# A new order of turns for a gated linear attention kernel with an MLP

## The chip, the cores and the metric

One core of a Trainium2 chip runs the kernel. Its engines are TensorE (PE in the profile, its weight loads PEld), VectorE (DVE), ScalarE (ACT), GpSimd (POOL) and SyncE (SP), which here issues nearly all DMAs. Each engine works off its own queue of instructions in the order in which the program emits them; semaphores make one wait for another. The metric is the device time of one execution in microseconds, the median of several runs.

## The reference

Two blocks, one after the other, in float32 (the weights come as float64):

```python
for t in range(S):            # B=4, H=8, S=768, D=48
    state = alpha[:, :, t, :, None] * state + einsum('bhd,bhe->bhde', k[:, :, t], v[:, :, t])
    y[:, :, t] = einsum('bhd,bhde->bhe', q[:, :, t], state)
x = y.transpose(0, 2, 1, 3).reshape(B, S, H * D)      # (4, 768, 384)
xn = (x - mean) / sqrt(var + 1e-6) * g_ln
out = x + maximum(xn @ w_ch1, 0) @ w_ch2              # 384 -> 1536 -> 384
```

## The kernel before

The sequence of 768 steps is cut into six chunks of 128 rows; with the four batches that makes 24 pieces of attention, called tokens here and lettered a to x (chunk 0 is a to d, chunk 1 e to h, and so on). The work of a token is a Python generator, `attention(c, b)` from L294: its instructions are emitted in pieces, each ended by a `yield`. Every other part of the kernel is a generator as well. One piece of a generator is a turn. The order of the work is a string, ORDER, of 1508 letters, and this loop at the end of the kernel is all that schedules it:

```python
with tc.manual_schedule():
    for turn in ORDER:
        next(turns[turn], None)
```

Each letter runs the next turn of its generator. Since engines take their instructions in order of emission, the string fixes the order on every engine, SyncE's DMA issues included, and with it which buffer each tile gets: buffers rotate among a few (six PSUM banks of tag "bank" for nearly all results of TensorE, seven buffers for raw inputs, eleven of tag "sum"), and a tile that takes a used buffer waits for its last reader.

The letters:

- **a to x**, the tokens. In order: issue loads of q, k, v (first chunk alone; later ones are loaded by an earlier token at L135, L141, L153 and L169); logarithm of alpha (ScalarE, L308); running sums by a triangular matmul (TensorE, L313, L316 or, for a later token, L403); two exponentials (ScalarE, L320); products with k and q (VectorE, L323, L325); the row of gates to DRAM (L330). Then q and k are transposed: in chunks 0 and 1 by TensorE (L351) with copies, from chunk 2 on by VectorE (L362) and a way through DRAM, four issues out (L368, tile td) and four back (L375, tiles kT and qT). Then the scores (TensorE, L393 or L401), their mask (VectorE, L407 or L413), the gates back from DRAM (L419), the sums of k times v (TensorE, L428), the state (VectorE L441, GpSimd L443), the outputs (TensorE, L454 or L459 and L463), their copy to x (ScalarE, L474 or L486, with VectorE L482 or L489), x to DRAM (L498), the layer norm (ScalarE, for chunk 0 VectorE L511), and its transpose: TensorE (L522) up to chunk 3, VectorE (L528) and DRAM (L532, L535) after that.
- **A to L**, twelve pieces of the weights: a load (L203), then three steps on VectorE, one on ScalarE (L223) and more on VectorE (L225 to L232), which turn float64 into float32.
- **Y, Z, P, Q**, the MLP of chunk 0: 12 hidden products for each half of the batches (L558, ReLU at L561), and the second products (L570, L574).
- **S, W, X, N**, sums and differences of blocks on VectorE (L800 of w1, L634 of w2, L825 of the normalised x, L661 of the hidden values), for chunks 1 to 5, whose two matrix products are made with fewer block products than the plain ones.
- **1 and 2**, the first product of chunks 1 to 5: 15 block products for each half of the hidden rows. An even turn is the matmuls (L848), the next reads the PSUM bank: one step on VectorE or ScalarE, and for some of them one or two late additions on GpSimd (L867 to L887). **R and U** are the ReLUs of the two halves (ScalarE, L898).
- **M**, the second product: 20 block products for each of the five chunks, turn by turn matmuls (L674) and reading (L684, L687, and late additions on GpSimd at L690), with the result sent to DRAM (L549) as it is ready. **O** loads x back from DRAM for the residual (L545).

A turn that waits holds up everything that stands behind it on its engine. So TensorE, which has the most work, waits when an operand is late, or when the bank that it is to write has not been read.

Of the kernel before, what the change touches and what calls it, by code (L numbers as in the profile page):

```python
# [30 lines left out]


ORDER = (
    "baabaccacdaadaabcacdbbbaaacbbbbcefdcabacccaabcdefabeafAbaBeebfefcaccedbcebCaaeea"
    "ddAdcbcgdabdeccBdbhedeggfbfgagdfgaCfcbhfddfgccdghdbhhedhbhgddAhehdedgiccfefdfgjA"
    "ijhchigYBYiCZYfjBiBZhfZZYZiYfiZefYgZjZCYkfgYeEZADihgDgjjjYDfZeEegZDgijefCYfYheEZ"
    "lYgigGYihijZGYefFZYlEkefGZFkhghYfFSZZYijZYljkFZeHYeihHYggkYllGHlYZfZhZglZeIlSQSh"
    "hYiSJQYkggkHISgiJSgISlmkmIfPjnJfkSKPZlnjjnnQnhPjnnLhhlOPKjKkLklLkhnOmkWkkOWhQhOk"
    "PSljmmQhmmpjmXkSSiPXSjoWnlQQKjXkiPikmSjpXWk1Q2inlk1WXSXWoXm2olSmmnmpoX121Xooj2km"
    "p2oom21j1nmp112k122Xjq212k1SOWm2p11p2Olpj22P22kmWmi2nn1lrml2j1k21nWjm11ll1Si1n12"  # L40
    "1p1kRUWnomR22rnp2Xq2n1pn2OUrrrRoUooo1ooqlrrMM12N11opomMpotWmpMrnq21lMmqRlNqqlpUq"
    "mpRoM1NUs2iN2MMoorNMMNlMNpMmsMONMMqMpRrlWMNWNMtMUrMiNtqqqqMtrtttstXMNMMvMnMsNMss"
    "tNM1MoiMpiqqiMsqMONXMNXMsMXXMMMOMn12qXtXor2tqXs2qprrov121X1qrX1oputr1v1p22pvv2pu"
    "12MrssssvXrv2s2noru12oss2s21ts21nus121JvO22Uux2pnu1u12u121v1R2U121Rt2us2t1xw2OU1"
    "1Rn112ssNpt1trM2pR22sMuv1uuwuwRtrvstsN2XNrM1MMNUMUNx1MMxNNRwwNMvMM1XwtXMwNtUMMMM"
    "qqMMNwMXNMMMMMNMxrMNMqXONM2MMNxXNMwMXMxrMMMMXMXMXt2112u22q2tu21s2uvwt2xuv2xuMt22"
    "2ruw222wtv21111qr1wxwxXwsv2x1xswu1Uw1t221q1121v12112U1R12xvO1Rxw1121OUq121RURxMq"
    "2wM2211NMrxxNMUu1MMtXxRMvNXxMMNxN2M2XNNNMMMONwXMvUMRNxMwuNMuMMMMMNMwXvMMMNwMvMMN"
    "MOXMXMvXwMNxM1NMXMMMMw22222xO221x1122Xu1222v1u2121211111X1Ux2Ov2112112111R122211"
    "1v2w2211RUUMUu211R222XN2RMU2XMMXX1X1RXMXMMMXNMMN11RM1NX12NMNN1121N111U1O1X2M2NNM"  # L50
    "N2111XMMM1MMLMNR12N22121M11MM1M111MMM2M22NNM2MMN222M212MU2M2MRM12RU2MOOMM222M1OR"
    "2UMNMUMMM1NMURNMM2NMNNNNMN2OMNMMMUMMMRMMMNMMMMMNMMMNMMMNMMNMMMNMMMMM"
)


# [904 lines left out]
```

## Time and profile before

| | |
|---|---|
| median of 3 runs | 424.13 us (422.38 to 424.32) |
| profiled execution, its own time | 422.32 us |
| its span, first to last instruction | 420.5 us |
| TensorE busy | 409.4 us, 4608 matmuls |
| VectorE busy | 351.7 us |
| ScalarE busy | 178.0 us |
| GpSimd busy | 152.1 us |
| DMA | 61.26 MB, mean 146 GB/s |
| clock granted to TensorE | 1.00 |

The span is what the profiler records between the first and the last instruction; the profiled execution's own time is 1.8 us longer. Each matmul in float32 stands as two in the counts. The end of a matmul is modelled by the profiler, so gaps between TensorE's instructions are read from the list of waits and from the chain of work that ended last, rather than from the busy share alone.

### The profile page before, as it was taken

The page shows a single profiled execution, that of the slowest core. Times are in us where ns is not written, and L with a number is a line of the kernel's source. Part 1 is how long each engine was busy: PE and PEld are TensorE (multiplying, and loading weights), DVE is VectorE, ACT ScalarE, POOL GpSimd, SP SyncE. Part 2 cuts the span into 40 slices and gives each one's busy share as a digit, 9 for nine tenths or more (in the row PEclk, how much of TensorE's full clock was granted, in tenths as well). Part 3 has the DMA queues.
Part 4 walks back from the last instruction along what each step waited for, and adds up shares of the span by engine and source line. Part 5 has one row for each costly group of instructions (what it writes and reads, how often), then busy time and mean ns, then how long its engine had stood idle before and what let it go on. Part 6 is the DMA issues. An engine that isn't in the chain of part 4 may idle for free.

```text
span 420.5 us, 11553 instructions
## 1 busy us (share of the span) xinstructions
PE 409.4 (97%) x4608; PEld 361.1 (86%) x4608; DVE 351.7 (84%) x713; ACT 178.0 (42%) x440; POOL 152.1 (36%) x164
## 2 busy tenths in 40 slices
PE   7998999999999999999999999999999999999997
PEld 5887888766678889898889998888998899999996
DVE  4999999999999999977798985787975789856773
ACT  6598356654055476227456315224623233103210
POOL 1021111000304990133396033683151951369114
PEclk9999999999999999999999999999999999999999
DMA  8999899899768788586776234642017110002101
GB/s 267 320 294 308 205 259 302 237 200 199 194 181 201 190 170 211 102 229 170 166 171 156 40 98 105 123 117 76 1 59 154 44 48 2 0 19 82 51 20 56
DMA packets 135037, 61.26 MB, mean 146 GB/s; under 512 B 90908, under 2 KB 131100, under 8 KB 134984
## 3 DMA queue, kind: packets, MB, share of 16 engines
q1 hardware_dynamic: 134440, 60.37, 56.0%
q8 instruction: 36, 0.59, 0.6%
q10 hardware_dynamic: 544, 0.17, 0.2%
q14 instruction: 17, 0.14, 0.1%
HBM read 43.12 MB, written 17.39 MB: 144 GB/s over the span
## 4 chain that ended last, share of the span: by engine, by line
PE 77%; DMA 9%; DVE 7%; SPq 4%; issue 2%; ACT 1%; POOL 1%; DVEq 0%; ACTq 0%; POOLq 0%
PE ops L674 30%; PE hps L848 28%; PE ops L570 6%; DMA vn<-in_v_dram 2%; PE aps L401 2%; PE yps L459 2%; PE sums L428 2%; SPq L375 2%; PE yps L463 1%; DMA rq<-in_q_dram 1%; PE tps L351 1%; DMA gate<-row 1%; DMA ws<-in_moe_w_ch_dram 1%; SPq L368 1%; PE aps L393 1%
## 5 line engine op out<-in xcount | busy, mean ns | idle before, releaser
L690 POOL TENSOR_TENSOR ob<-ob,u 128x192 f32<-128x192 f32 x40 | 26.4, 670 | 81.7 <-DVE ob L687 62.2
L848 PE MATMUL hps<-sum,w 128*128 128x256 f32 x192 | 46.1, 381 | 0.0
L443 POOL TENSOR_TENSOR mid<-mid,gate 112x192 f32<-112x192 f32 x20 | 12.8, 640 | 89.9 <-DVE mid L441 70.8
L898 ACT ACTIVATE hT<-hT 128x512 f32<-128x512 f32 x48 | 28.9, 626 | 33.6 <-POOL hT L870 16.2
L848 PEld LDWEIGHTS hps<-sum,w 128*128 128x128 f32 x192 | 36.1, 190 | 4.9
L674 PE MATMUL ops<-w,hT 128*128 128x192 f32 x224 | 40.3, 326 | 0.0
L674 PEld LDWEIGHTS ops<-w,hT 128*128 128x128 f32 x224 | 37.1, 190 | 0.5
L848 PE MATMUL hps<-xT,w 128*128 128x256 f32 x136 | 34.6, 381 | 1.0 <-ACT x L474 1.0
L570 PE MATMUL ops<-w,hT 128*128 128x384 f32 x96 | 33.0, 491 | 0.0
L558 PE MATMUL hps<-xT,w 128*128 128x256 f32 x144 | 32.7, 383 | 0.0
L674 PE MATMUL ops<-ws,sum 128*128 128x192 f32 x160 | 29.2, 329 | 1.5 <-ACT x L486 1.5
L558 PEld LDWEIGHTS hps<-xT,w 128*128 128x128 f32 x144 | 26.9, 190 | 3.9
L848 PEld LDWEIGHTS hps<-xT,w 128*128 128x128 f32 x136 | 25.2, 190 | 4.4 <-ACT x L474 1.4
L674 PEld LDWEIGHTS ops<-ws,sum 128*128 128x128 f32 x160 | 26.3, 190 | 2.4 <-ACT x L486 1.8
L570 PEld LDWEIGHTS ops<-w,hT 128*128 128x128 f32 x96 | 17.7, 190 | 10.7
L684 DVE TENSOR_TENSOR ob<-ops,ob 128x192 f32<-128x192 f32 x50 | 17.6, 352 | 10.4 <-PE ops L674 5.7
L674 PE MATMUL ops<-ws,hT 128*128 128x192 f32 x128 | 23.7, 328 | 0.0
L459 PEld LDWEIGHTS yps<-st,qT 48*64 48x64 f32 x320 | 20.0, 134 | 3.9 <-issue 2.1
L463 PE MATMUL yps<-vx,at 64*64 64x48 f32 x320 | 23.0, 219 | 0.0
L463 PE MATMUL yps<-vn,at 64*64 64x48 f32 x320 | 22.5, 220 | 0.0
L459 PE MATMUL yps<-st,qT 48*64 48x48 f32 x320 | 22.1, 220 | 0.1
L674 PE MATMUL ops<-more,sum 128*128 128x192 f32 x120 | 22.0, 326 | 0.0
(248 smaller groups left out, 1115.7 us busy)
## 6 DMA issues: line engine op xcount, KB each, us to landing
ws<-in_moe_w_ch_dram SPq DMA_DIRECT2D x12, 768.0 KB, 6.0
td<-tr SPq DMA_DIRECT2D x64, 96.0 KB, 2.8
vn<-in_v_dram SPq DMA_DIRECT2D x12, 384.0 KB
kept<-x SPq DMA_DIRECT2D x24, 192.0 KB, 4.3
ob<-kept SPq DMA_DIRECT2D x24, 192.0 KB, 2.5
out_dram<-ob SPq DMA_DIRECT2D x19, 192.0 KB, 2.5
ra<-in_alpha_dram SPq DMA_DIRECT2D x16, 192.0 KB, 2.5
kT<-td SPq DMA_DIRECT2D x32, 96.0 KB, 4.4
```

The source lines that it names most:

```text
L375: nc.sync.dma_start(t[64 * i:64 * i + D].rearrange("r p s t -> r p (s t)"), td[n, :, i].rearrange("p d t -> d p t"))
L401: nc.tensor.matmul(to, kT[rs, p, s], qT[rs, p, s], start=True, stop=True)
L443: nc.gpsimd.tensor_mul(new, new, by)
L459: nc.tensor.matmul(yps[i][halves[s], i, p], qT[rs, p, s], (now, mid)[s][rs, p], start=True, stop=r != i)
L463: nc.tensor.matmul(yps[r][halves[s], i, p], at[halves[r], p, s], by, start=r != i, stop=True)
L558: nc.tensor.matmul(hps, w1[:, j // 2, f, j % 2 * P:][:, :P], xT_of[0][:, f, bs], start=(f == 0), stop=(f == NF - 1))
L570: nc.tensor.matmul(ops_of[b], hT_of[c][:, j, b], w2[:, j], start=(j == 0), stop=(j == NJ - 1))
L674: nc.tensor.matmul(acc, lhs[:, j], rhs[:, j], start=(j == 0), stop=(j == NT - 1))
L684: nc.vector.tensor_add(x, acc, x)
L690: getattr(nc.gpsimd, f"tensor_{op}")(x, x, y)
L848: nc.tensor.matmul(acc[:, i], w, b, start=True, stop=True)
L898: nc.scalar.activation(out=x, in_=x, func=AFT.Relu)
```

## The change

The change replaces the string ORDER by another with the same 1508 letters, each as often as before. No function, buffer, transfer or instruction is added or taken away. The two strings agree letter by letter in 74 places; a turn is moved by 12 places on average, the farthest by 359. Both strings end on turns of M, N and a few others.

```diff
 ORDER = (
-    "baabaccacdaadaabcacdbbbaaacbbbbcefdcabacccaabcdefabeafAbaBeebfefcaccedbcebCaaeea"
-    "ddAdcbcgdabdeccBdbhedeggfbfgagdfgaCfcbhfddfgccdghdbhhedhbhgddAhehdedgiccfefdfgjA"
-    "ijhchigYBYiCZYfjBiBZhfZZYZiYfiZefYgZjZCYkfgYeEZADihgDgjjjYDfZeEegZDgijefCYfYheEZ"
-    "lYgigGYihijZGYefFZYlEkefGZFkhghYfFSZZYijZYljkFZeHYeihHYggkYllGHlYZfZhZglZeIlSQSh"
...
-    "1Rn112ssNpt1trM2pR22sMuv1uuwuwRtrvstsN2XNrM1MMNUMUNx1MMxNNRwwNMvMM1XwtXMwNtUMMMM"
...
-    "2UMNMUMMM1NMURNMM2NMNNNNMN2OMNMMMUMMMRMMMNMMMMMNMMMNMMMNMMNMMMNMMMMM"
+    "bacabcadaacbcaadbcadabcababbebaccbadbaaBbccaedcbceAeeaaacbfecfBcdafddeaedbdeafae"
+    "bcdccbfgadhAdcgCcdbebeebfhggdfgbfffbCdcgfgecdfchgdfhgabcddchdhAiiegjhacehedhhjfg"
+    "biAdfidAeBhBijffYYiCjZZYYifZYlZCgjYDlYYjjZZYBZYgDieEgDgDjZZekEhZYGZgZigZGeeYgYgg"
+    "fZYEhfGfkChihiYFYijfgEhgkhFZYhgYfghijgkFeZZlGZShfZYHlhHfYFYZeZHelYiZgllPmZkJIgJk"
...
+    "Us1pXqU11x2tO2MM1vwMUM12xuRvu1vurNNNNwtOuuMwRxvNtxRNutwwMM2MOwNXwMNuXMMtNM1rMMMw"
...
+    "MNM1MMOMRMNMUUM2ONMNNNMO2MMMUMNMMMMMRMMNNMMMNMNMMNMMMMMMMMNMNMMMMMMM"
 )
```

More of the change, by code (lines that the diff above doesn't have):

```diff
@@ L33 @@
 ORDER = (
-    "baabaccacdaadaabcacdbbbaaacbbbbcefdcabacccaabcdefabeafAbaBeebfefcaccedbcebCaaeea"
-    "ddAdcbcgdabdeccBdbhedeggfbfgagdfgaCfcbhfddfgccdghdbhhedhbhgddAhehdedgiccfefdfgjA"
-    "ijhchigYBYiCZYfjBiBZhfZZYZiYfiZefYgZjZCYkfgYeEZADihgDgjjjYDfZeEegZDgijefCYfYheEZ"
-    "lYgigGYihijZGYefFZYlEkefGZFkhghYfFSZZYijZYljkFZeHYeihHYggkYllGHlYZfZhZglZeIlSQSh"
-    "hYiSJQYkggkHISgiJSgISlmkmIfPjnJfkSKPZlnjjnnQnhPjnnLhhlOPKjKkLklLkhnOmkWkkOWhQhOk"
-    "PSljmmQhmmpjmXkSSiPXSjoWnlQQKjXkiPikmSjpXWk1Q2inlk1WXSXWoXm2olSmmnmpoX121Xooj2km"
@@ L40 @@
[L40 to L44, printed above, removed]
-    "1Rn112ssNpt1trM2pR22sMuv1uuwuwRtrvstsN2XNrM1MMNUMUNx1MMxNNRwwNMvMM1XwtXMwNtUMMMM"
@@ L46 @@
[L46 to L51, printed above, removed]
@@ L52 @@
-    "2UMNMUMMM1NMURNMM2NMNNNNMN2OMNMMMUMMMRMMMNMMMMMNMMMNMMMNMMNMMMNMMMMM"
+    "bacabcadaacbcaadbcadabcababbebaccbadbaaBbccaedcbceAeeaaacbfecfBcdafddeaedbdeafae"
+    "bcdccbfgadhAdcgCcdbebeebfhggdfgbfffbCdcgfgecdfchgdfhgabcddchdhAiiegjhacehedhhjfg"
+    "biAdfidAeBhBijffYYiCjZZYYifZYlZCgjYDlYYjjZZYBZYgDieEgDgDjZZekEhZYGZgZigZGeeYgYgg"
+    "fZYEhfGfkChihiYFYijfgEhgkhFZYhgYfghijgkFeZZlGZShfZYHlhHfYFYZeZHelYiZgllPmZkJIgJk"
+    "PeiYjJIflHeSZIQgkIlYSjiPkffennSQlOKjLSnSjmSQhKnSjLnKPkiljnhSQnLkkjkWknkShOmPhkhl"
@@ new lines @@
+    "kOOhWlmmphmQmkmXjWQnXjlSQjPmkilXSXkP2OXWjXQjkjW2iXoSWX2oWX22Pi2mnol1j1mom2omSpoo"
+    "l1XSpk2oW2m112p1m2pm11m1W211pp12O122r22jnn21lpnmnjSml1riOn2l12Rl111kqS1m21W1Rkp2"
+    "o21mUXpq1mU2rUrnmj1rl2Rno2oomqonrormpokO1rNM2Mipin1op1ionoqUM2qp2W12RkMmNqiMoRtk"
+    "UrpkqNM1NoMliMlNUMMNMNMKNqMlNorMWrnmtltNRMsqppMWNMriMMMpNlsqqqnoqttNttMtMsXMMssM"
+    "sMNMNMX1oXXppMvstM2MXMMNMsppXoMXoqMsMMXM1nqqv11Xq1trMq2tqX21rn12v1r2ur2r222rvsqs"
+    "svsu1rs1nuvvt2s11ss11p22rtsvosn2uropuXru222221uts212stnU1211u1121222Op1Rp2tRU21R"
@@ new lines @@
+    "Us1pXqU11x2tO2MM1vwMUM12xuRvu1vurNNNNwtOuuMwRxvNtxRNutwwMM2MOwNXwMNuXMMtNM1rMMMw"
+    "qtXMMMxNUNxtMMsNMMMxXxMtXtrMMqMNrMXNvutMMwNuMMMNMMMxMLMOM11vvuq2X2O2wMus1wX11222"
+    "2r2Xt1222w22utsqxvw2x2ww1vx21sX12121xwvq2O2x2w111u1uvU121w12s1wuRvx12U11J1q21R1U"
+    "OvRxU121wMMu2xxsRNMw2NNMRM1MUNN2MMuUMqXN1MrNNRMNvMXNXMMMM2MMMxNM1uNXMMNMNMOXMXMv"
+    "MMXOMMMXxNxwxMMvNMMMMMXMx21w1x222212v12w222x122w2212X11UX2212121121121wx111MU11X"
+    "2RR2v1211212211R1URU211XOUM2XNRX1MX1RM2MXN2MXNXNMXXMXMMMN111U1MN1M1122MNM1MM2MM1"
@@ L53 @@
+    "11NNN121O11NM1MM21N1112N1122M1MMM12MM12N222M22M2RM1M2N22MM2MU1ON2M22M2UURR22RNNM"
+    "MNM1MMOMRMNMUUM2ONMNNNMO2MMMUMNMMMMMRMMNNMMMNMNMMNMMMMMMMMNMNMMMMMMM"
 )
```

## The prediction

> **What bounds the kernel now.** I read the page first, then the busy time by stretch, then TensorE's own waits, then the chain and the engines' timelines around each wait.
>
> ```profile
> span 420.5 us, 11553 instructions
> PE 409.4 (97%) x4608; PEld 361.1 (86%) x4608; DVE 351.7 (84%) x713; ACT 178.0 (42%) x440; POOL 152.1 (36%) x164
> ...
> PEclk9999999999999999999999999999999999999999
> ```
>
> TensorE has 11.1 us of idle time in 420.5, at full clock throughout. The change touches no instruction, so the 409.4 us stay, and only these 11.1 us, and what a new order adds to them, can move. The stretches (columns: window, length, busy time of each engine, clock, DMA share, GB/s) say where they lie:
>
> ```profile
> 0.00:20.00 20.00, 17.07 (x176) 13.11 (x176) 13.37 (x36) 11.11 (x25) 2.04 (x6) 1.00 0.93 303
> 20.00:180.00 160.00, 155.91 (x2372) 128.10 (x2373) 155.19 (x290) 86.88 (x219) 41.06 (x43) 1.00 0.85 216
> 180.00:400.00 220.00, 218.94 (x1960) 202.86 (x1959) 172.06 (x362) 78.59 (x194) 102.58 (x105) 1.00 0.37 91
> 400.00:420.50 20.50, 17.52 (x108) 17.03 (x106) 11.05 (x28) 1.47 (x3) 6.46 (x10) 1.00 0.11 39
> ```
>
> 2.9 us at the start, 3.0 at the end, 4.1 from 20 to 180 us, 1.1 after that. From 20 to 180 us VectorE (third figure) is as full as TensorE: 155.2 against 155.9 of 160 us. Behind 180 us VectorE has 22% to spare. TensorE's waits by name:
>
> ```profile
> PE xps L522 <- DVE xn L511: 1.9, 1, 1.9
> PE ops L674 <- ACT x L486: 1.5, 1, 1.5
> PE lps L250 <- DVE more L247: 1.1, 1, 1.1
> PE hps L848 <- ACT x L474: 1.0, 1, 1.0
> PE lps L313 <- ACT la L308: 1.0, 2, 0.5
> PE tps L351 <- DVE qk L325: 0.9, 1, 0.9
> ```
>
> The third, fifth and sixth are the start (first loads, first transpose), about 3.0 us. The other three, 1.95, 1.50 and 1.03 us, are what an order can win. The chain shows what the 1.50 comes from:
>
> ```profile
> 173.28 4.19 DMA ra<-in_alpha_dram
> 177.49 0.52 ACT la L308
> 178.02 0.20 ACT few L514
> 178.24 0.71 ACT xn L515
> 178.94 0.38 ACT x L486
> 179.33 0.04 issue
> 179.37 1.57 PE ops L674 x8
> ```
>
> A load of alpha took 4.19 us. ScalarE stood at its Ln, and behind the Ln stood the copy of x that frees a PSUM bank for the next product. And the 1.03 us:
>
> ```profile
> 284.90 1.23 POOL hT L886
> 286.14 0.02 issue
> 286.16 0.04 ACT hT L898
> ...
> 286.70 0.61 ACT hT L898
> 287.31 0.34 ACT x L474
> 287.66 0.04 issue
> 287.70 1.13 PE hps L848 x4
> ```
>
> GpSimd's late additions hold two ReLUs on ScalarE, and the copy of x that frees the bank stands behind them.
>
> **The change part by part.** I write k8 for the turn of token k with count 8, from 0. Against each string I count the TensorE work ahead of a turn: 1.30 us for a product of eight matmuls at L674, 0.86 for four at L848, 1.29 for six at L558, 2.58 for eight at L570 (all rows of the chain), and a token's small turns likewise. This is a place in the queue, not a time.
>
> *Loads of alpha, k, q (L169) ahead of their Ln.* Before, the load for s stands 0.3 us of TensorE work ahead of s0, that for o 0.8, that for v 1.3 (the wait above); the median of the twelve is 6.0. After, the smallest two are 2.6 (m, r), the next 7.4 (v), the median 11.1. Against the 4.19 us of the row, the wait at 177 us goes: gain 1.50, bounds 0 (the bank comes late for another reason) and 1.50. I take 1.5. Next late there is the load for r: its issue can run ahead of its place by some 3 us, as SP did before (below), and I charge nothing; without that cover it costs 4.2-2.6 = 1.6.
>
> *ReLUs and GpSimd (U15, R15, x16).* Before, turn 1-85 stands ahead of 2-85, so U15 waits for the third of four additions, and U15 and R15 both stand ahead of x16. After, 2-85 comes first, and x16 stands behind U15 but ahead of R15. Two GpSimd additions of 1.23 and 1.27 us are no longer ahead of U15, so the bank comes 2.5 us earlier: gain 1.0, bounds 0 and 1.03.
>
> *The transposes at 31 us (b21, C1, b22).* Before, C1's three VectorE steps (0.56, 0.96 and 1.32 us rows) stand ahead of the xn that b22 transposes. After, b21 stands ahead of C1, but c23's xn stands behind it and behind two more steps, with c24 as its reader. VectorE's timeline has no gap from 23.8 to 44.0 us, and the same VectorE work stands ahead of the first hidden product Y0 in both orders (counted to A3, which ended at 39.0 us). So the wait moves: gain 0.3, bounds 0 and 1.95, nearer to 0 for that reason.
>
> *v loads (L141) ahead of sums (L428).* The one that held TensorE for some 0.3 us at 122 us (j20 to m12; the chain has 4.73 us of DMA vn there) goes from 4.7 to 6.4 us. f21 to i12 goes from 11.8 to 3.4. Gain 0.3 less nothing, bounds -1.3 and 0.3.
>
> *kT and qT loads (L375) ahead of the scores (L401).* This part goes against the change. The smallest places were 2.5 (i), 2.6 (p), 3.2 (m); now they are 1.5 (u), 1.7 (p), 2.2 (v), 2.6 (k), 3.4 (q). These loads take:
>
> ```profile
> DMA to landing us min/median/max: 3.5/4.4/5.2
> ```
>
> Places below 4.4 did not hold TensorE before: p's four issues stood 2.6 ahead of scores that began at 146.4, so their place was 143.8, but SP's timeline has them from 141.62 to 143.6: SP came 2.2 ahead of its place, and no wait of TensorE is listed. Walking SP's queue in the new order, each issue at its row's duration, each wait at the time before of what it waits for: u and v land some 3 us ahead of use, p 0.4 and m 0.6 behind, w 1.6 behind (w8 now stands behind x7's four issues and still behind the send M67, which waits for GpSimd). Cost 0 to 2.6; I take 1.0, since the same walk puts j before at 0.9 behind and TensorE was not held there.
> [...]
>
> *Switches of tile.* TensorE goes from full-size to half-array matmuls and back 29 times against 27. By the starts of the matmuls in the trace, a switch costs 0.09 us and the return 0.14 us. Cost 0.5, bounds 0 and 0.5.
>
> *VectorE's work placed earlier.* At 35 us of TensorE work the new order has 6.1 us more VectorE work ahead (C3, D0, j6; while g11 and h11, which free banks, come 7 and 12 us later); at 157 us 3.9 more, at 232 us 2.7 more; at 55 and 75 us 3 less. What waits behind: releases of PSUM banks. Cover: the other five banks, 1.3 us of product each, and at 232 us VectorE's 22% of spare time. Cost 0 to 6.1+3.9 = 10; I take 0.3, nearest to the rows of before, where bank releases by VectorE held TensorE for no listed wait over 0.5 us.
>
> Start and end: the last turns are products and VectorE additions in both strings, and the first loads carry the same bytes; 0.
>
> Sum: -1.5 -1.0 -0.3 -0.3 +1.0 +0.5 +0.3 = -1.3 us. The profiled execution took 422.32 us, so 421.0. It lies 1.8 under the median 424.13, at the low end of the three (422.38 to 424.32). On the median: 422.8 us, -0.3%, which is inside the 0.5% (2.1 us) that a measurement of this kernel can tell from no change.
>
> **The rivals.**
>
> *All waits go, nothing comes.* SP keeps its lead, so kT costs 0, and the wait at 31 us is halved. -1.5 -1.03 -1.0 -0.3 +0.3 = -3.5: 420.6 us. For it: seven of the twelve alpha loads are now over 10 us ahead. Against: VectorE's gapless rows at 31 us.
>
> *VectorE holds the banks (the other side).* Place: 35 and 157 us of TensorE work, 46 and 170 us of the span, where VectorE is 97% busy. If TensorE's next product needs a bank whose reader stands behind the work moved ahead, TensorE waits until VectorE has caught up: 6.1 and 3.9 us less the cover of about 2.6 us (two spare banks) each, 3.5+1.3 = 4.8; with the other terms at -1.3, +3.5: 427.6 us. It decides from the point where the excess outgrows the free banks' cover, about 4 us of VectorE work for the sum to leave the 0.5%. For it: VectorE has 4.8 us of idle time in these 160. Against: at 45 and 165 us both orders have the same VectorE work ahead, within 0.5.
>
> *The DMA waits only change their place.* kT costs its full 2.6 and r 1.6: +1.6: 425.7 us.
>
> *The clock.* The longest gap of TensorE is 1.95 us and the granted clock 1.00 throughout; if a new kT wait were as long as a whole landing (4.4) and the clock halved for as long behind it, 4.4 and 2.2 lost on top of the sum: 429.4 us. The Trainium skill, page "TensorE: Matmul & The Clock Gate", section "The HAM clock gate", has the clock drop to half after about 3.4 us of idleness; no gap of this trace is long enough to show it, and by that rule too the clock stays where waits stay under that.
>
> **How the numbers follow.** Chances: the sum holds 0.40 (within 2 us of 422.8; 0.14 of it lies below 422.0), all gains 0.19, VectorE 0.27, moved DMA waits 0.10 (0.08 within 0.5%), clock 0.04. Faster: 0.14+0.19 = 0.33. Slower: 0.27+0.02+0.04 = 0.33. Same: 0.26+0.08 = 0.34. The likeliest one's own range is 420.8 to 424.8. For 8 in 10 the range goes down to the rival of all gains with its other bound (the full 1.95 at 31 us, 1.0 more: 419.6, and 0.6 for the scatter), 419.0, and up to VectorE's with 0.9 of scatter, 428.5.
>
> **What would show it.** TensorE's waits: no line "ops L674 <- ACT x L486" of 1.5 and no "hps L848 <- ACT x L474" of 1.0; "xps L522 <- DVE xn" still there, at c24. New lines at aps L401 at some 257 us (w), 145 (p) or 121 (m) would show the kT step. ScalarE's wait for alpha (10.3 us in total before, of which the start has 5.8) falls to some 6. VectorE as the bound shows as TensorE waiting for VectorE's L413, L684 or L882 near 46 and 170 us. TensorE busy well off 409.4 us would say that the matmuls themselves are paced otherwise, which I have not reckoned with; it, or waits spread over many places under 0.2 us, would make the prediction wrong.

## The result and the profile after

| | before | after |
|---|---|---|
| median, 6 runs of each | 424.42 us (422.38 to 425.47) | 420.46 us (419.70 to 420.96) |
| profiled execution, its own time | 422.32 us | 420.14 us |
| its span | 420.5 us | 418.3 us |

The ratio is 0.9909, 95% interval 0.9885 to 0.9934: faster by 0.9%. The forecast of 422.8 us, no measurable change, is 2.3 us too high: the time lies inside the stated range of 419.0 to 428.5 us, and 0.3 us under what the likeliest case alone allowed (420.8 to 424.8). It is the number of the rival "all waits go, nothing comes" (420.6 us), but not its mechanism: that rival had a net 3.5 us of waits go, and 2.6 went. That the two times agree is luck. Two things have to be explained: the 2.2 us between the two spans, and why the medians lie further apart (4.0 us). One execution of the kernel after, the profiled one of e5 below, took 1486.56 us where the others took 420 to 424, its matmuls at L848 starting 0.84 us apart in place of 0.216; why is open, and it is left out everywhere, with e5's trace.

The page of the kernel after, span, busy time and the granted clock in 40 slices:

```profile
span 418.3 us, 11560 instructions
PE 409.8 (98%) x4608; PEld 361.3 (86%) x4608; DVE 351.4 (84%) x713; ACT 177.5 (42%) x440; POOL 151.6 (36%) x164
...
PEclk9999999999999999999999999999999999999999
```

TensorE is as busy as before within 0.4 us, so what went is idle time. The stretches of the kernel after (window, length, busy time of each engine, clock, DMA share, GB/s):

```profile
0.00:20.00 20.00, 17.30 (x173) 13.31 (x174) 13.62 (x35) 10.83 (x23) 2.04 (x6) 1.00 0.94 307
20.00:180.00 160.00, 157.30 (x2381) 129.14 (x2380) 154.50 (x292) 88.54 (x225) 39.41 (x43) 1.00 0.85 217
180.00:400.00 220.00, 220.00 (x1965) 204.03 (x1964) 174.18 (x367) 77.85 (x192) 104.01 (x106) 1.00 0.37 89
400.00:418.30 18.30, 15.15 (x94) 14.86 (x92) 9.14 (x22) 0.32 (x1) 6.16 (x10) 1.00 0.12 43
```

From 20 to 180 us TensorE idles 2.7 us instead of 4.1, from 180 to 400 us not at all. The start and the end idle as before, about 3 us each. TensorE's waits in the kernel after (total, times, longest):

```profile
PE lps L313 <- ACT la L308: 1.6, 2, 1.4
PE xps L522 <- DVE xn L511: 1.5, 1, 1.5
PE lps L250 <- DVE more L247: 1.1, 1, 1.1
PE yps L459 <- ACT x L486: 0.6, 1, 0.6
PE sums L428 <- DVE st L441: 0.2, 1, 0.2
```

The waits of 1.5 us at L674 and 1.0 us at L848 are gone, the one at the transposes (L522) is 0.4 us shorter, and there is no line for kT or qT (L401) and none for a bank that VectorE holds. One wait is new, 0.6 us for ScalarE's copy of x. The list adds up to 5.0 us against 7.6 before, 2.6 us less, beside spans that differ by 2.2. In the chain of the kernel after the new wait stands between two outputs:

```profile
114.34 0.06 PE yps L463
114.40 0.02 issue
114.42 0.50 ACT x L486
114.92 0.04 issue
114.97 0.25 PE yps L459
```

Turns k17 and i17, both outputs, stand next to each other there, and the second needs the bank that the copy of the first frees.

A finer reading than the list is TensorE's lag: when a matmul starts, less the work ahead of it. Work is counted with one fixed start-to-start time for each kind of matmul, taken from the trace of before (0.163 us at L674, 0.216 at L848 and L558, 0.323 at L570 and so on; 402.7 us in all, the same for every order). How much the lag grows between two amounts of work shows where an order loses time, whatever the clock on the wall says there. In us:

| TensorE work | before | before again (e1) | after | after again (e9) | v0 early (e10) | both moves (e4) |
|---|---|---|---|---|---|---|
| 0 to 25 | 4.68 | 4.42 | 4.53 | 4.75 | 4.56 | 4.85 |
| 25 to 60 | 3.25 | 4.58 | 3.30 | 3.16 | 3.20 | 3.51 |
| 60 to 100 | 0.27 | 0.59 | -0.19 | -0.33 | -0.32 | 0.31 |
| 100 to 155 | 1.32 | 1.85 | 2.65 | 3.67 | 2.52 | 1.47 |
| 155 to 180 | 1.32 | 1.07 | -0.54 | -0.53 | -0.54 | -0.15 |
| 180 to 260 | 1.99 | 2.06 | 2.46 | 2.47 | 2.47 | 3.30 |
| 260 to 285 | 1.94 | 1.93 | 0.38 | 0.38 | 0.38 | 0.62 |
| 285 to the end | -0.28 | -0.27 | -0.47 | -0.47 | -0.47 | -0.28 |
| sum | 14.49 | 16.23 | 12.12 | 13.10 | 11.80 | 13.63 |

The columns with e1, e9, e10 and e4 belong to experiments below. Between before and after the 2.4 us come from two places, 1.9 us at 155 to 180 and 1.6 us at 260 to 285, plus 0.5 at 60 to 100; 1.3 us are given back at 100 to 155 and 0.5 at 180 to 260. Nothing here says what the 0.5 at 60 to 100 and the 0.5 at 180 to 260 are.

### The profile page after: what moved, and what is told of

Its sections match the earlier page's. It is cut to its first block, busy times and chain, and to the rows that moved or that the text cites. A ratio compares the mean times of both kernels' runs of the same rounds, so it can differ in the third digit from the quotient of the medians.

```text
span 418.3 us, 11560 instructions
## 1 busy us (share of the span) xinstructions
PE 409.8 (98%) x4608; PEld 361.3 (86%) x4608; DVE 351.4 (84%) x713; ACT 177.5 (42%) x440; POOL 151.6 (36%) x164
## 4 chain that ended last, share of the span: by engine, by line
PE 89%; DVE 4%; DMA 2%; ACT 2%; issue 1%; POOL 0%; POOLq 0%; SPq 0%; DVEq 0%
PE hps L848 31%; PE ops L674 30%; PE ops L570 8%; PE hps L558 7%; PE aps L401 3%; PE yps L459 2%; PE yps L463 2%; PE sums L428 2%; DMA vn<-in_v_dram 2%; PE xps L522 1%; PE aps L393 1%; DMA ra<-in_alpha_dram 1%; PE lps L313 1%; DVE w L217 1%; PE tps L351 1%
## 5 line engine op out<-in xcount | busy, mean ns | idle before, releaser
L848 PE MATMUL hps<-sum,w 128*128 128x256 f32 x192 | 46.3, 381 | 0.0
L443 POOL TENSOR_TENSOR mid<-mid,gate 112x192 f32<-112x192 f32 x20 | 11.6, 580 | 81.8 <-DVE mid L441 51.3
L674 PE MATMUL ops<-w,hT 128*128 128x192 f32 x224 | 40.5, 327 | 0.0
L848 PEld LDWEIGHTS hps<-sum,w 128*128 128x128 f32 x192 | 36.1, 190 | 5.0
L674 PEld LDWEIGHTS ops<-w,hT 128*128 128x128 f32 x224 | 37.1, 190 | 0.7 <-issue 0.2
L848 PE MATMUL hps<-xT,w 128*128 128x256 f32 x136 | 34.0, 380 | 0.0
L570 PE MATMUL ops<-w,hT 128*128 128x384 f32 x96 | 33.0, 492 | 0.0
L558 PE MATMUL hps<-xT,w 128*128 128x256 f32 x144 | 32.5, 382 | 0.0
L558 PEld LDWEIGHTS hps<-xT,w 128*128 128x128 f32 x144 | 27.0, 190 | 4.2
L674 PE MATMUL ops<-ws,sum 128*128 128x192 f32 x160 | 28.7, 327 | 0.0
L848 PEld LDWEIGHTS hps<-xT,w 128*128 128x128 f32 x136 | 25.5, 190 | 3.1
L570 PEld LDWEIGHTS ops<-w,hT 128*128 128x128 f32 x96 | 17.5, 190 | 10.8 <-DVE w L232 0.4
L674 PEld LDWEIGHTS ops<-ws,sum 128*128 128x128 f32 x160 | 26.5, 190 | 0.3
L443 POOL TENSOR_TENSOR st<-st,gate 112x192 f32<-112x192 f32 x16 | 11.6, 725 | 35.6 <-DVE st L441 25.9
L674 PE MATMUL ops<-ws,hT 128*128 128x192 f32 x128 | 23.6, 328 | 0.0
L401 PEld LDWEIGHTS aps<-qT,kT 48*64 48x64 f32 x576 | 19.1, 134 | 4.1 <-issue 0.8
```

The lines of the kernel that those rows point to most:

```text
L401: nc.tensor.matmul(to, kT[rs, p, s], qT[rs, p, s], start=True, stop=True)
L443: nc.gpsimd.tensor_mul(new, new, by)
L558: nc.tensor.matmul(hps, w1[:, j // 2, f, j % 2 * P:][:, :P], xT_of[0][:, f, bs], start=(f == 0), stop=(f == NF - 1))
L570: nc.tensor.matmul(ops_of[b], hT_of[c][:, j, b], w2[:, j], start=(j == 0), stop=(j == NJ - 1))
L674: nc.tensor.matmul(acc, lhs[:, j], rhs[:, j], start=(j == 0), stop=(j == NT - 1))
L848: nc.tensor.matmul(acc[:, i], w, b, start=True, stop=True)
```

## The experiments

In all of them the only edit is in the string ORDER. Times are medians of 12 executions (e5: 11, e9: 6); the ratio is to the kernel before, which ran on the same chip beside them. They ran in three groups, each on one chip: e1 to e4 (before: 424.12 us), e5 to e8 (424.20 us), e9 to e12 (425.3 us).

### e1: the kernel before again

No edit; it shows what two runs of one order differ by.

> The kernel before, unchanged, for its scatter and a second profile. The medians moved by 4.0 us, the two profiles by 2.2 only. If the first profile of before was a lucky execution (theory A), this one has a span over 421.5 us and TensorE waits that the first one lacks, for DMAs above all, with over 8.5 us of waits in place of 7.6. If executions differ in the pace of TensorE and not in waits (rival), the list of waits stays as it was and the busy time is up. Ratio 1.000 either way, within 0.002.

424.06 us, ratio 1.0011 [0.9979, 1.0042]: no difference, as expected. Its profiled execution took 424.07 us, 1.75 more than the profile on which the forecast stands, and not by its waits, which add up to 7.4 us against 7.6. TensorE is busy for 411.7 us instead of 409.4, so it is the rival's case, the pace of TensorE. Its busy times and some of its waits:

```profile
PE 411.7 (98%) x4608; PEld 363.1 (86%) x4608; DVE 351.8 (83%) x713; ACT 178.3 (42%) x440; POOL 151.6 (36%) x164
...
PE xps L522 <- DVE xn L511: 1.9, 1, 1.9
...
PE aps L401 <- DMA qT<-td: 0.5, 2, 0.3
```

and two stretches of the same execution, the clock third from the end:

```profile
30.00:34.00 4.00, 1.88 (x45) 1.36 (x42) 3.93 (x8) 3.64 (x12) 0.11 (x1) 1.00 0.82 214
34.00:38.00 4.00, 4.00 (x54) 3.67 (x55) 3.06 (x8) 2.98 (x6) 1.06 (x1) 0.57 0.92 318
```

TensorE has 1.88 us of work in 4.00, and then its clock is 0.57 over the next 4: the trace has it at half from 34.15 us on, for 3.41 us. By the table the lag grows by 1.33 us more at 25 to 60 than in the first profile of the same order. And the old order too waits for kT and qT, 0.5 us in two places, where the first profile shows none.

### e2, e3, e4: the two waits removed from the kernel before

e2 moves v0, the logarithm of v's alpha, behind i26 and p18; e3 moves U15 and R15, the two ReLUs, behind x16; e4 does both:

```diff
-...MMvMnMsNMsstNM1MoiMpiqqiMsq...
+...MMMnMsNMsstNM1MoiMpiqqivMsq...
```

```diff
-...R1Rw1121OUq121RURxMq2wM2211NMrxxNMUu1...
+...R1Rw1121OUq121RxMq2wM2211NMrxURxNMUu1...
```

> Before, with the one turn v0 (the Ln that waited for alpha at 177 us) put behind the copy of x that frees the bank (p18) and behind i26. Theory of the prediction: the wait of 1.5 us (ops L674 <- ACT x L486) goes and the time falls by 1.5 us, ratio 0.9965 (0.995 to 0.998). Rival, the bank comes late for another reason: ratio 1.000, and a wait of over 1 us near 178 us under another name.

> Before, with the two ReLU turns U15 and R15 put behind the copy of x (x16) that they held up. Theory: the wait of 1.0 us (hps L848 <- ACT x L474) at 287 us goes, ratio 0.9976 (0.996 to 0.999). Rival, GpSimd's lateness holds the next turns instead: ratio 1.000, with a wait of TensorE for L898 or L661 within the next 10 us.

> Both moves of the two runs above in one kernel. Theory, the two add up: -2.5 us, ratio 0.994; then 1.5 us of the changed kernel's gain lies elsewhere. Rival, these two waits carry all of it: -3.5 us or more, ratio 0.992 or lower. Second rival, they do not add (one wait hides behind the other): -1.5 us, 0.9965.

| | median | ratio to before |
|---|---|---|
| e2, v0 later | 423.83 us | 0.9992 [0.9967, 1.0016] |
| e3, ReLUs later | 423.19 us | 0.9962 [0.9936, 0.9988] |
| e4, both | 422.04 us | 0.9951 [0.9924, 0.9977] |

In each trace the wait aimed at is gone. e4's list begins

```profile
PE xps L522 <- DVE xn L511: 1.9, 1, 1.9
PE sums L428 <- DVE st L441: 1.1, 2, 0.7
```

and no wait for ScalarE's x stands in it, at L674 or at L848. e4 gains 2.1 us of the 2.5 expected. The whole change ran beside the old order on another chip (e5 and e9 below); against those two ratios the two moves bring some 0.4 to 0.7 of it. Singly, e2 gives 0.3 us (1.5 expected, which lies just outside its interval) and e3 0.9 by the medians, 1.6 by the ratio (1.0 expected). So in e2 the wait went and the time hardly moved; why is open. With intervals of 1 us to either side, only the sum of the two is told from nothing with ease. e2's profiled execution had the half clock at 34 us too, and its lag at 155 to 180 fell by 0.6 us, where before's grew by 1.32. e3's profiled execution lost 1.9 us at a place that the edit doesn't touch. Its chain there:

```profile
155.24 0.80 DVE hT L661
156.03 2.41 issue
158.45 0.68 DVE hT L889
159.12 0.28 DVE st L441
```

On VectorE's timeline the step at L661 took 3.37 us there; the same step took 0.68 us in before and in e1, which have the same turns up to there. The chain counts 2.41 us of it as time in which nothing that the profile shows was waited for, and TensorE's sums waited behind it. The cause is open.

### e5 and e9: the kernel after again

> The changed kernel, unchanged, beside the others on one chip. Theory (its gain is the three waits of its profile and the start, 2.2 us by the spans): ratio 0.994 to 0.995. Rival (before loses some 1.5 us more in most executions to late DMAs, which one lucky profile of it did not show): ratio 0.990 to 0.992, and times that scatter less than those of before.

> The kernel after itself, as the base of the three next to it. Theory (the waits removed are the gain, 2.2 to 2.7 us of 424): ratio to the kernel before 0.993 to 0.995. Rival (the spread shown first, 0.9909, is the size): 0.990 to 0.992.

e5: 421.46 us, 0.9931 [0.9897, 0.9964]; its times reach from 420.26 to 423.72 us. e9: 421.21 us, 0.9886 [0.9846, 0.9925]. e5 lies between the two expectations and e9 below both; with the first, 0.9909, they don't settle whether the gain is 0.6% or 1.1%. e9's trace, by TensorE's timeline, has a wait that the first profile of this order hasn't:

```profile
122.54 0.24 PE L401 MATMUL aps<-qT,kT 48*64 48x64 f32 x1 [0.87 <-DMA qT<-td]
```

These are the scores of m and n, whose kT and qT were issued at 112.5 to 118.6 us. e9's span is 419.3 us, and the table has the 1.0 us at 100 to 155.

### e6 and e7: the new order up to a point, the old one behind it

e6 keeps the first 299 letters of the new string (62 us of TensorE work), e7 the first 1075 (255 us); the letters left over follow in the old order.

```diff
 # e7, the line of the seam
-    "2r2Xt1222w22utsqxvw2x2ww1vx21sX12121xwvq2O2x2w111u1uvU121w12s1wuRvx12U11J1q21R1U"
+    "2r2Xt1222w22utsqxvw2x2ww1vx21sX1212JsxswUw121q112112112U1R12xv1Rxw1121OUq121RURx"
```

> The new order up to the turn at 62 us of TensorE work (299 letters), then the old order of what is left. Theory: only the start and the wait at 31 us are better, -0.7 us, ratio 0.998; the waits of 1.5 and 1.0 us are there as before. Rival (the first 62 us, where most DMA traffic is, carry the gain that the profile of before does not show): ratio 0.995 or lower.

> The new order up to the turn at 255 us of TensorE work (1075 letters), then the old order of what is left. Theory: all gains but the ReLU one, ratio 0.9965 by the spans, with the wait of 1.0 us at 287 us (hps L848 <- ACT x L474) there as before. Rival (late DMAs between 62 and 255 us carry the rest): ratio 0.992 to 0.993.

e6 was a miss: 426.37 us, 1.0039 [1.0005, 1.0073], slower than either order. Its waits show what the seam made:

```profile
PE lps L313 <- ACT la L308: 2.5, 2, 1.9
PE xps L522 <- ACT xn L515: 2.1, 1, 2.1
...
PE sums L428 <- DMA vn<-in_v_dram: 1.0, 1, 1.0
```

The wait of 2.1 us for ScalarE's xn is in neither whole order: here the seam of two orders cost more than the new beginning gained. e7 came as expected, 422.64 us, 0.9964 [0.9933, 0.9995], with the wait of 1.0 us at L848 still listed and that at L674 gone.

### e8: the new wait at 114 us taken away

i17 is moved behind P6, so that it no longer follows k17 at once.

```diff
-...SQjPmkilXSXkP2OXW...
+...SQjPmklXSXkPi2OXW...
```

> The changed kernel with one turn moved: i17 (outputs of token i) put behind P6 (eight second products of chunk 0), so that two tokens' outputs no longer follow each other directly. Theory: the wait of 0.6 us at 114 us (yps L459 <- ACT x L486) is for a bank that ScalarE frees after the first token's copy, and 2.6 us of products cover it: -0.6 us against the changed kernel, ratio to before 0.0015 below that of the changed kernel. Rival: P's banks are missed instead, no difference.

421.76 us, 0.9931 [0.9893, 0.9969], 0.3 us from e5 on the same chip: the times can't tell 0.6 us from nothing. In the trace the theory holds: the wait is gone, and from 69 us on no wait of TensorE over 0.2 us is left. A wait of the same size is new in its list, but elsewhere:

```profile
PE sums L428 <- DMA vn<-in_v_dram: 0.6, 1, 0.6
```

TensorE's timeline has it 46 us ahead of the turn that was moved:

```profile
68.24 0.57 PE L428 MATMUL sums<-vn,qk 64*48 64x48 f32 x32 [0.63 <-DMA vn<-in_v_dram]
```

These are the sums of i (i12), waiting for the load of v that f21 issues. e7 has 0.26 us there and e12 0.56; the first profile of after, e9, e10 and e11 have none. All but e12 have the same turns up to there, so this wait comes and goes by execution.

### e10: v0 put back in the kernel after

The logarithm of v's alpha goes right behind t5, which issues its load: nearer to it than in the old order, where eight turns stand between.

```diff
-...qnoqttNttMtMsXMMssMsMNMNMX1oXXppMvstM2M...
+...qnoqttNtvtMtMsXMMssMsMNMNMX1oXXppMstM2M...
```

> The order after with one letter put back: v0, the logarithm of v's alpha, right behind t5, some 1.3 us of TensorE work behind the issue of its load, as before. Theory: the load of 4.2 us holds ScalarE, the copy of x behind it frees the bank late, and a wait of TensorE of about 1.5 us comes back at some 176 us: ratio to the order after in the same runs 1.0035. Rival (the gain comes from the order elsewhere, and the bank would be late by another cause or not needed): 1.000, no such wait.

The theory failed: no such wait. 421.78 us, 0.9913 [0.9877, 0.9950], against 421.21 us of the unchanged order beside it, and the profiled span is the shortest of all, 418.0 us. ScalarE's timeline in e10 (start, duration, in brackets what it was idle for):

```profile
174.92 0.52 ACT L308 ACTIVATE la<-ra 128x384 f32<-128x384 f32 x1 [3.22 <-DMA ra<-in_alpha_dram]
...
176.97 0.47 ACT L486 ACTIVATE x<-yps 128x384 f32<-128x384 f32 x1
```

and TensorE in the chain of the same stretch:

```profile
174.23 5.40 PE ops L674 x32
179.62 0.86 PE hps L848 x4
```

ScalarE does wait, 3.22 us, for the load. But the load was issued at 172.38 us and had landed by 174.92, 2.54 us; in the first profile it took 4.21 (173.28 to 177.49). So the copy of x that frees the bank ends at 177.44 instead of 179.32, and TensorE goes through its four products without a stop. The place of v0 was not the whole cause of the old wait; the other part was how long that load took. That is not the chance of one execution. In the three other traces that have v0 in its old place (e1, e3 and e6) the chain has the same load:

```profile
175.09 4.06 DMA ra<-in_alpha_dram
```

```profile
177.16 3.71 DMA ra<-in_alpha_dram
```

```profile
177.45 4.41 DMA ra<-in_alpha_dram
```

TensorE waited 1.4, 1.0 and 1.7 us behind it. What differs beside v0 is what SyncE issues next. Before, then e10:

```profile
173.28 0.39 SPq L169 DMA_DIRECT2D ra<-in_alpha_dram  x1
174.77 0.35 SPq L169 DMA_DIRECT2D rk<-in_k_dram  x1
```

```profile
172.38 0.39 SPq L169 DMA_DIRECT2D ra<-in_alpha_dram  x1
175.21 0.33 SPq L169 DMA_DIRECT2D rk<-in_k_dram  x1
```

In the old order the loads of k and q follow 1.5 and 2.0 us behind that of alpha, while it is on its way; in e10 that of k comes 2.8 us behind, when alpha has landed. That they slow it is argued, not shown, and whether the bank is needed as early in the new order was not separated either.

### e11: p's loads of kT and qT behind o's

p8 goes behind o8, past four issues on SyncE's queue.

```diff
-...l1XSpk2oW2m...1Rkp2o21mUXpq1...
+...l1XSpk2oW2m...1Rk2op21mUXpq1...
```

> The order after with p8 (the four loads of p's kT and qT) put behind o8's four instead of ahead of them; on SyncE's queue that is some 1.9 us later, and nothing else moves. In the trace of the order after p's last issue is at 142.2 us and its scores start at 145.4; these loads land 2.3 to 4.6 us behind their issue, median 3.4. Theory (what counts is the time that SyncE runs ahead, and here it has about none to spare): TensorE waits for qT 1.5 to 2.0 us at 145 us, ratio to the order after 1.004 to 1.005. Rival (kT loads cost nothing within 2 us, as the forecast's failed term would have it): 1.000, no wait at L401.

422.84 us, 0.9935 [0.9904, 0.9966], 1.6 us above the unchanged order beside it. TensorE's timeline in e11:

```profile
147.01 0.30 PE L401 MATMUL aps<-qT,kT 48*64 48x64 f32 x2 [0.58 <-DVE sum L825]
148.24 0.24 PE L401 MATMUL aps<-qT,kT 48*64 48x64 f32 x1 [0.94 <-DMA qT<-td]
```

and its chain there:

```profile
144.73 0.30 SPq L375
145.04 0.04 issue
145.08 3.03 DMA qT<-td
148.11 0.14 issue
148.24 0.24 PE aps L401
```

The first is put down to a VectorE step, the second to the load; the unchanged order has neither, and together they are 1.5 us, the low end of what was expected. So kT's place is not free: it cost nothing in the traces in which SyncE ran ahead of it, and in the new order p has less than 2 us to spare.

### e12: more VectorE work ahead of a bank

D0, D1 and D2, 4.3 us of VectorE work on a piece of the weights, go ahead of g11, the mask that reads a bank of scores.

```diff
-...YYifZYlZCgjYDlYYjjZZYBZYgDieEgDgDjZZ...
+...YYifZYlZDDCDgjYlYYjjZZYBZYgieEggDjZZ...
```

> The order after with D0, D1 and D2 (4.3 us of VectorE work on a piece of the weights) ahead of g11, the mask that reads a bank of scores; in the order after they stand partly behind it. It doubles the VectorE work that the new order has ahead at 35 us of TensorE work. Theory: no wait; the bank that g11 reads is next needed later than that, and VectorE's total up to the next product is the same: ratio to the order after 1.000. Rival (VectorE holds the banks, 4.3 us less a cover of 2.6): a wait of TensorE of about 1.7 us between 45 and 55 us, ratio 1.004.

423.62 us, 0.9959 [0.9928, 0.9990], 2.4 us above the unchanged order. VectorE's timeline in e12 has a wait for D's load at D0:

```profile
46.47 0.56 DVE L215 TENSOR_SCALAR w<-ws 128x768 int32<-128x768 int32 x1 [1.35 <-DMA ws<-in_moe_w_ch_dram]
```

The chain of e12 has that load:

```profile
39.73 6.72 DMA ws<-in_moe_w_ch_dram
```

And TensorE's timeline in e12, some microseconds later:

```profile
50.15 2.83 PE L558 MATMUL hps<-xT,w 128*128 128x256 f32 x12 [1.15 <-DVE w L229]
```

Neither theory: no bank was late. D's load took 6.72 us, VectorE stood at D0 for it, and the weights of C behind D0 came late for a hidden product. The run therefore doesn't measure how much VectorE work the banks would bear. It shows how little room D0 has: its load was issued at 38.81 us in the first profile of after, with D0 at 47.36. With the 6.72 us of this run it would have landed at 45.53, so by this estimate D0 could stand 1.8 us earlier, and the edit asked for more.

## Why the prediction was right and wrong

**The two waits (-1.5 and -1.0): right in place, mechanism and nearly in size.** The wait at 287 us is 1.6 us in the lag, and e3 removed it from the old order by putting the copy of x ahead of both ReLUs (the new order has it ahead of one). The wait at 177 us is 1.9 us in the lag. In the new order the logarithm of v stands behind the copy of x that frees the bank (177.14 and 176.77 us on ScalarE), so its load can't hold that copy any more, and ScalarE waits 5.6 us for alpha in total instead of 10.3, as forecast. e2 removed the wait by v0's place alone. e10 shows that this place was one of two causes: with v0 back, the load itself came sooner. The forecast took the 4.19 us as given in the new order as well.

**The transposes at 31 us (-0.3): the wait is 0.4 us shorter, and by the lag at 25 to 60 nothing is gained.** VectorE has 9.9 us of work in each of the two tens from 20 to 40 us in both orders, so it sets the pace there, as argued.

**The loads of v (-0.3): a gain and a cost that was put at nothing.** No trace of the new order has a wait of m12 for its load (e1 has 0.25 us there), so that gain came. For f21 to i12, which went from 11.8 to 3.4, the sum charged nothing, with 1.3 us as the bound; e7, e8 and e12 wait 0.26, 0.63 and 0.56 us there, the other four traces nothing.

**kT and qT (+1.0): the term that failed in the first profile, where it is 0.** One step of it was misread: the row of 3.5/4.4/5.2 us is that of the tile kT alone. The tile qT is issued last and so sets when the scores can start. The same trace has both (the last figure is the median time to landing):

```profile
kT<-td SPq DMA_DIRECT2D x32, 96.0 KB, 4.4
qT<-td SPq DMA_DIRECT2D x32, 96.0 KB, 3.2
```

With 3.2 in place of 4.4 the walk of SyncE's queue would have had p and m in time, j before in time too, as TensorE showed, and w 0.4 us late instead of 1.6 (an estimate from these two medians). The other executions show the rest. e9 has 0.87 us, e11 0.62 and e12 0.51 at m and n, at 122 to 125 us; the walk had m late by 0.6 at 121. For w, where it had 1.6, no trace shows a wait (the scores of w start at 256 us), and for p, where it had 0.4, only e11 does, with 1.5 us when its loads are put 2 us later. But before isn't free of it either: e1 has 0.5. So the term should have been a difference between two orders that both sometimes wait, some 0 to 0.5, not 1.0 against 0.

**Switches of tile (+0.5) and VectorE's work placed earlier (+0.3).** No listed wait of TensorE for a bank that VectorE holds appears in any trace of the new order, so the second is 0, and the rival "VectorE holds the banks" fell with it. The lag at 100 to 155 grows by 1.3 us more than before; the new wait at 114 us is 0.6 of them, and the rest agrees with the switches in size, though no run separated it.

**From the profile to the median (+1.8): the step that failed most.** The forecast took 421.0 us for the profiled execution, where it was 420.14 (and 421.08 in e9), and added the 1.8 us by which the median of before lay above its profile. The new order's median lies 0.3 us above its profile, and 0.1 in e9; but it lies 1.5 above in e8 and 2.0 in e10, which differ from it by one turn. So the 1.8 was no property of an order that could be carried over: it says which execution was profiled. The old order's first profile was as short as its quickest execution. Quickest against quickest, the two orders differ by 2.3 to 3.0 us in the three comparisons (422.38 and 419.70, 422.56 and 420.26, 423.27 and 420.26), which is near the 2.2 of the spans and the 2.6 of the waits; the medians differ by 2.7 to 4.1. (The old order ran more often in two of them, which gives it more chances of a quick execution.)

What makes the old order's other executions longer stays open. The traces have one candidate. In 66 of 99 executions of the kernel before, the mean granted clock is under 0.999, against 7 of 71 of the kernel after and its variants (the first six, e5, e8 to e12). In e1 that was the half clock from 34.15 us on, and it cost 1.3 us of lag. In the emptiest 3.4 us around 30 to 35 us TensorE has 1.3 to 1.5 us of work in the old order and 1.7 to 1.8 in the new. So the clock, which the last of the rivals had fall in the new order, may have fallen in the old one, and the change would have taken that away. Against it: in the three groups the executions of the old order with the lower clock have medians of 424.3, 424.4 and 425.2 us, those without 424.1, 424.0 and 425.7, so there is no difference in one direction. And e4, which keeps the old beginning, has the lower clock in 9 of 12 and is 2.1 us quicker. Only the lowest clocks go with long times: six executions at 0.987 to 0.992 took 427.5 to 429.5 us (a seventh, longer still, is left aside), too few to move a median. A run with the old start of the string ahead of the new order would tell more; it was not tried.

**A slip in a rival.** With kT's full 2.6 and r's 1.6, "the DMA waits only change their place" adds up to +1.9 and 426.0 us, not +1.6 and 425.7.

## What to carry to other kernels

A move that only reorders is to be read at the waits of TensorE one by one: two waits named in the profile, each with the instruction that stands ahead of the release, gave about half of this gain by three moved letters. A transfer's duration in one trace is not a constant. Part of it belongs to the order: the load of alpha took 3.7 to 4.4 us in four traces of one order and 2.5 in another. Part of it belongs to the execution: the load of v held i12 in two of six traces with the same turns. So what it costs to stand closer to a reader is a chance of a wait, in both orders. Read the row of the transfer that lands last, not that of its neighbour. Before a sum made on a profile is carried to the median, ask whether that profile is an ordinary execution, and take a second one.

## What the runs showed of the hardware that was not expected

The start of TensorE's full clock differs by execution, not by order: in the clock records it comes 4.36 us behind the span's start in e4, 5.22 in after, 9.83 in e2 and 14.02 in e7. The same four matmuls at L313, in after and then in e7:

```profile
5.08 1.61 PE L313 MATMUL lps<-la,consts 128*128 128x384 f32 x4 [0.25 <-ACT la L308]
```

```profile
5.36 2.93 PE L313 MATMUL lps<-la,consts 128*128 128x384 f32 x4 [0.53 <-ACT la L308]
```

Both have the same turns there. The first scores start at 11.39 us in after and 15.11 in e7: 3.7 us, more than the 2.2 between the two spans of the result, are decided before the order matters.
The Trainium skill, page "TensorE: Matmul & The Clock Gate", section "The HAM clock gate", describes a window of 3.4 us that runs free of the kernel, so that the moment of full clock varies. The spell of 3.41 us in e1 agrees with that window, and so does its place: the drop comes 27.31 us behind the rise to full clock in e1 and 23.89 in e2, eight and seven times 3.41. The section also has the clock drop after an idle window of that length; here the clock fell with no gap of TensorE over 1.95 us, so a whole idle window was not needed.

In windows of 3.41 us counted from the rise of the clock, the one just ahead of the drop holds 1.33 us of TensorE work in e1 and 1.63 in e2. In the first profile of before and in e4 the clock stayed up: the same empty stretch falls across two windows, and no window of theirs holds less than 2.13 and 1.83 us. So which executions of one order lose clock agrees with how the stretch lies to the windows. A limit can't be read off: e6 has a window of 1.63 us too, and no drop behind it.
